# Local attention and a top-2 mixture of experts on one core: the normalisation after the product with v moves from VectorE to ScalarE and POOL, the row stores move to the sync queue, and the later steps come one turn later

## The chip, the core and the metric

The kernel runs on one core of a Trainium2 chip. The core has TensorE (PE; its weight loads are shown apart as PEld), VectorE (DVE), ScalarE (ACT), GpSimd (POOL) and SyncE (SP), which here only issues DMAs. Each engine works through its own list of instructions in order; DMAs are issued from the queues of SP, ACT and POOL. The metric is the device time of one execution in microseconds (us), the median of the runs.

## The reference

The inputs q, k, v have 8 batches, 8 heads, 576 positions and 64 values per head. Attention is local: each chunk of 64 positions attends to itself alone.

```python
scores = scale * np.matmul(q_c, k_c.transpose(0, 1, 2, 4, 3))
scores = scores - np.max(scores, axis=-1, keepdims=True)
attn = np.exp(scores)
attn = attn / (np.sum(attn, axis=-1, keepdims=True) + 1e-09)
out = np.matmul(attn, v_c)
```

The result, as 4608 token rows of 512 values (x), goes to a mixture of 8 experts. A noisy gate (`x @ w_gate + log1p(exp(x @ w_noise)) * noise`) picks two experts for each token and gives them softmax weights; each expert computes `relu(x @ w1[e]) @ w2[e]` on its tokens, and the weighted results are added to the output rows.

## The kernel before, in words

**Attention.** The 4608 tokens are 36 tiles of 128. One call of `attend(it)` is one turn, and it works on several tiles at different steps. For tile t: `scores` (turn t) makes 32 small products of 64x64 in PSUM; `soft_max`, `soft_sub` (DVE) take the row maximum and subtract it, `soft_exp` (ACT) takes the exponential in place; `p_trans` (turn t+2) transposes the result on PE and ACT copies it to SBUF (tile `pts`); `pv` (turn t+3) multiplies by v in 32 small products into PSUM banks 3 and 4. A column of ones beside v gives the row sums, so each head has 65 columns. In turn t+4 the DVE normalises: `norm_a` adds 1e-9 to the 8 sums (L440), `norm_b` takes their reciprocals (L443), `norm_c` multiplies the 512 columns by them, from PSUM into the SBUF tile `xs` (L447). `x_trans` (turn t+5) issues the store of `xs` to the DRAM buffer `xbuf` from ACT's queue, transposes `xs` on PE (L455), and ACT copies the result (L456). Every four tiles `gate_mm` and `gate_sum` make the gate's logits, in the same PSUM banks 3 and 4, beside pv's product. The softmax leaves out the division, which `norm_c` does at the end.

**Order.** The program is written out by hand: the order of the calls in `attend` is the order of the instructions on each engine, and the framework adds the waits. In one turn the order is `p_trans`, `x_trans`, gate, `scores`, `norm_a/b/c`, route steps, `soft_max`, route steps, `soft_sub`, route steps, `soft_exp`, `pv`. Loads of q, k and v come through SP, several tiles ahead.

**Routing.** `route(g)` is a generator that chooses the experts for a group of 4 or 8 tiles and builds the experts' token lists. `step_route(n)` runs n of its steps, ten in a turn, so its small DVE, ACT, POOL and PE instructions lie between those of attention. Its last part makes, for each tile, one-hot matrices (`gohp` on POOL and ACT at L596 to L598, `geq` on DVE at L600, `grhs` on POOL at L604) and adds them up by matmuls (`place`, L588). When a group is done, `gather` fetches the rows of `xbuf` that one of the first three expert blocks needs (POOL queue, L236).

**Experts.** 24 blocks of up to about 400 tokens: `layer1` and `layer2`, each product as three fp32r matmuls of high and low parts (L301). The turns after the last scores (`tail`) run as hooks between the matmuls of the first block's `layer1`. In `layer2` of block 0 the hook turns the tokens of block 1 (`x_tile`, transposes at L284), fixed at its seventh group of three matmuls per tile. The output buffer is set to zero by 37 stores of 256 KB from SP (`zero_out`, L666), which must have landed before the first expert's result is added to it (L268).

Weights for expert 0 are split into high and low parts in eight of the turns (its 10, 11, 13, 14, 16, 17, 19, 20): ACT makes the high part (L135), POOL the low part (L136).

Of the kernel before, what the change touches and what calls it, by code (L numbers as in the profile page):

```python
# [8 lines left out]
FT = mybir.dt.float32  # L9
# [4 lines left out]
AF = mybir.ActivationFunctionType  # L14
OP = mybir.AluOpType
# [4 lines left out]
P = 128  # L20
NTOK = 4608
NT = NTOK // P
DM = 512
# [37 lines left out]
def kernel(ctx, tc, qT, kT, vh, wgn, noise, w1, w2, out, caps=CAPS):  # L61
    nc = tc.nc
# [4 lines left out]
    xbuf = dram.tile([NROWS, DM], FT, name="xbuf")  # L67
# [50 lines left out]
    def w_load(e, which, c):  # L118
        st = stage.tile([P, 1024], FT, name="st")
        staged[e, which, c] = st  # L120
        if which == 1:
            nc.sync.dma_start(st, w1v[ds(place[e], 1), c].rearrange("o j r f -> (o j) r f") if e else w1[e, c * P:(c + 1) * P, :])
        else:
            nc.sync.dma_start(st.rearrange("p (f n) -> p f n", f=2),
                              w2[ds(place[e], 1) if e else slice(0, 1), 2 * c * P:(2 * c + 2) * P, :]
                              .rearrange("o (f p) n -> p (o f) n", f=2))
# [295 lines left out]
    def p_trans(t):  # L422
        for hp in range(4):
            nc.tensor.transpose(PS[:, 2, hp * P:(hp + 1) * P], PR[t][:, hp * P:(hp + 1) * P], ident)  # L424
        PT[t] = work.tile([P, 4, P], FT, name="pts", bufs=3)
        nc.scalar.activation(PT[t].rearrange("p a b -> p (a b)"), PS[:, 2, :], AF.Copy)

    pvb = PS[:, 3:5, 0:260].rearrange("p b (g n) -> p b g n", n=65)
# [1 line left out]
    def pv(t):  # L430
        v = vb[t // 2]
        for hp in range(4):
            for h, c in HC:
                r, s = slice(h * 64, h * 64 + 64), slice(c * 64, c * 64 + 64)
                nc.tensor.matmul(PS[s, 3 + h, hp * 65:hp * 65 + 65], PT[t][r, hp, s], v[r, t % 2, c, hp, :],  # L435
                                 start=True, stop=True)

    def norm_a(t):
        RC[t] = work.tile([P, 2, 4, 1], FT, name="rc", bufs=2)
        nc.vector.tensor_scalar(RC[t], pvb[:, :, :, 64:65], 1e-9, None, op0=OP.add)  # L440

    def norm_b(t):
        nc.vector.reciprocal(RC[t], RC[t])  # L443

    def norm_c(t):
        XS[t] = work.tile([P, DM], FT, name="xs", bufs=4)
        nc.vector.tensor_tensor(by_head(XS[t]), pvb[:, :, :, 0:64], RC[t].to_broadcast([P, 2, 4, 64]), OP.mult)  # L447

    def x_trans(t):
        g, r = divmod(t, 4)  # L450
        if r == 0:
            XT[g] = gx.tile([P, ND, 4, P], FT, name="xt", bufs=1)
        nc.scalar.dma_start(xbuf[(t + 1) * P:(t + 2) * P, :], XS[t])
        for d in range(ND):
            nc.tensor.transpose(PS[:, 5, d * P:(d + 1) * P], XS[t][:, d * P:(d + 1) * P], ident)  # L455
        nc.scalar.activation(XT[g][:, :, r, :], PS[:, 5, :].rearrange("p (d n) -> p d n", d=ND), AF.Copy)  # L456
# [3 lines left out]
    def gate_mm(g):  # L460
        for d in range(ND):
            nc.tensor.matmul(PS[32 * d:32 * d + 32, 6, :], wg[:, d, :], XT[g][:, d], start=True, stop=True)  # L462
        LS[g] = gx.tile([P, 4, P], FT, name="ls", bufs=1)
        nc.scalar.activation(LS[g].rearrange("p a b -> p (a b)"), PS[:, 6, :], AF.Copy)
# [6 lines left out]
    def gate_sum(g):  # L471
        for r in range(4):
            nc.tensor.matmul(lg_at(4 * g + r), LS[g][:, r, :], sel, start=True, stop=True)  # L473
# [169 lines left out]
    def step_route(n):  # L643
        for _ in range(n):
            while routing:
                try:
                    next(routing[0])
                    break
                except StopIteration:
                    routing.pop(0)  # L650
# [17 lines left out]
    def attend(it):  # L668
        STEPS = 2 if it < 33 else 3
        if it % 2 == 0 and it >= 2 and it // 2 + 3 < NT // 2:  # L670
            load_q(it // 2 + 3)
            load_k(it // 2 + 3)
        if it in (4, 7, 10, 13):
            w_load(0, 1, (it - 4) // 3)
        if 0 <= it - 2 < NT:
            p_trans(it - 2)
        if 0 <= it - 5 < NT:
            x_trans(it - 5)
        if it - 7 >= 0 and (it - 7) % 4 == 3:
            gate_sum((it - 7) // 4)  # L680
        if it - 6 >= 0 and (it - 6) % 4 == 3:
            gate_mm((it - 6) // 4)
        if it < NT:
            scores(it)
        if 0 <= it - 4 < NT:
            norm_a(it - 4)
            norm_b(it - 4)
            norm_c(it - 4)
            step_route(3 * STEPS)
        if it - 7 >= 0 and (it - 7) % 4 == 3:  # L690
            if grp_of[it - 7] != grp_of.get(it - 6):
                routing.append(route(grp_of[it - 7]))
        if it < NT:
            mx = soft_max(it)
            step_route(STEPS)
            soft_sub(it, mx)
            step_route(STEPS)
            soft_exp(it)
        if 0 <= it - 3 < NT:
            pv(it - 3)  # L700
        if it % 2 == 1 and it >= 3 and (it - 3) // 2 + 4 < NT // 2:
            load_v((it - 3) // 2 + 4)
        if it in (10, 11, 13, 14, 16, 17, 19, 20):
            w_split(0, 1, *wq.pop(0), eng=nc.gpsimd)
        if it in (29, 31, 33, 35):
            w_load(0, 2, (it - 29) // 2)
# [15 lines left out]
        x_tile(0, k)  # L722


    tail = [NT + 1 + a for a in range(6)]

    def hook_tail(f, d):
        if d == 0 and f % 2 == 0 and f >= 2:
# [212 lines left out]
```

## Time and profile before

| | |
|---|---|
| median of 3 runs | 1022.05 us (1020.68 to 1023.5) |
| the profiled execution | 1018.32 us, span 1016.4 us, mean granted TensorE clock 0.981 |
| PE busy | 968.3 us (95% of the span) |
| DVE, ACT, POOL busy | 461.4, 299.6, 484.6 us |
| first scores matmul | 5.66 us |
| first expert matmul | 154.30 us |
| first layer 2 matmul | 190.09 us |

In a row of the timeline the first number is the start in us from the span's start, the second the duration in us, then engine, line, operation, output and inputs; a bracket gives how long the engine had been idle before it and what ended that. A row of a table by windows gives, for each stretch, the busy us of PE, PEld, DVE, ACT and POOL (instructions in parentheses), then the granted clock, the DMA engines' busy share and GB/s. In a row of groups of instructions the last column before the bar is the count; after it stand the total us and the mean ns of one.

### The profile page before, as it was taken

What the parts mean: (1) busy time and instruction counts of PE and PEld (TensorE: products, weight loads), DVE (VectorE), ACT (ScalarE), POOL (GpSimd) and SP (SyncE); (2) the same over time, 40 slices, a digit from 0 to 9 for tenths busy, and PEclk for the clock granted to TensorE, in tenths of its full rate; (3) what the DMA queues carried; (4) which work ended last, traced back from release to release, by engine and by line L of the source; (5) the groups of instructions that cost most, each with busy time, mean ns of one, the idle gap of its engine ahead of it and who ended that gap; (6) DMA issues with size and microseconds to landing.
All of it is one profiled execution on the core that took longest, in us unless ns stands there. A gap on an engine that the chain in (4) does not pass through costs nothing.

```text
span 1016.4 us, 18332 instructions
## 1 busy us (share of the span) xinstructions
PE 968.3 (95%) x7353; PEld 865.4 (85%) x7353; DVE 461.4 (45%) x1037; ACT 299.6 (29%) x649; POOL 484.6 (48%) x618
## 2 busy tenths in 40 slices
PE   6878888999999999999999999999999999999995
PEld 5667766988889899989998999899989998899984
DVE  5577765554525353335334533453345334434311
ACT  3466653331414132213221322232223221323100
POOL 1133432434677777347724783487248725711111
PEclk9799978999999999999999999999999999999998
DMA  9988891133251553245224532353344234412213
GB/s 368 387 312 276 297 392 73 42 79 94 61 132 45 120 157 63 39 104 157 63 36 100 156 68 45 95 160 65 56 107 134 59 60 106 138 13 29 32 22 42
DMA packets 51943, 121.51 MB, mean 120 GB/s; under 512 B 8288, under 2 KB 9184, under 8 KB 51856
## 3 DMA queue, kind: packets, MB, share of 16 engines
q0 software_dynamic: 20160, 38.69, 20.4%
q1 hardware_dynamic: 26512, 72.20, 19.7%
q10 hardware_dynamic: 5184, 9.44, 2.4%
q8 instruction: 58, 0.95, 0.4%
q14 instruction: 29, 0.24, 0.1%
HBM read 81.56 MB, written 38.73 MB: 118 GB/s over the span
## 4 chain that ended last, share of the span: by engine, by line
PE 90%; DVE 5%; ACT 1%; issue 1%; DMA 1%; POOL 0%; SPq 0%; DVEq 0%; ACTq 0%; POOLq 0%
PE PS L301 79%; PE PS L588 2%; PE PS L435 2%; PE PS L408 2%; PE PS L424 2%; PE PS L455 1%; DMA kb<-in_kT 1%; DVE xs L447 1%; PE PS L330 1%; DVE mx L412 1%; DVE pr L417 1%; PE PS L473 1%; PE PS L462 1%; PE PS L284 0%; DVE xl L292 0%
## 5 line engine op out<-in xcount | busy, mean ns | idle before, releaser
L256 POOL DMA_INDIRECT xg<-xbuf,piece x257 | 265.8, 1034 | 71.7 <-issue 65.1
L301 PE MATMUL PS<-xh,w1h 128*128 128x384 f32 (+2 forms) x768 | 263.2, 343 | 2.4 <-DVE xl L292 1.4
L301 PE MATMUL PS<-xl,w1h 128*128 128x384 f32 (+2 forms) x768 | 260.6, 339 | 0.3 <-DVE xl L292 0.3
L301 PE MATMUL PS<-xh,w1l 128*128 128x384 f32 (+2 forms) x768 | 260.8, 340 | 0.0
L268 POOL DMA_INDIRECT out<-o,lid x73 | 116.9, 1601 | 238.9 <-DVE o L339 222.8
L301 PE MATMUL PS<-w2h,hh 128*128 128x512 f32 x584 | 228.7, 392 | 0.0
L301 PE MATMUL PS<-w2h,hl 128*128 128x512 f32 x584 | 227.7, 390 | 0.0
L301 PE MATMUL PS<-w2l,hh 128*128 128x512 f32 x584 | 227.5, 390 | 0.0
L319 ACT ACTIVATE hh<-PS 128x384 fp32r<-128x384 f32 (+1 forms) x192 | 93.9, 490 | 363.7 <-PE PS L301 363.7
L320 DVE SCALAR_TENSOR_TENSOR hl<-PS,hh 128x384 fp32r<-128x384 f32 (+1 forms) x192 | 107.2, 559 | 195.4 <-ACT hh L319 195.4
L339 DVE TENSOR_SCALAR o<-PS,lwt 128x512 f32<-128x512 f32 x73 | 54.7, 750 | 229.7 <-PE PS L301 229.7
L301 PEld LDWEIGHTS PS<-xh,w1h 128*128 128x128 f32 x768 | 144.6, 188 | 5.9 <-DVE xl L292 1.7
L301 PEld LDWEIGHTS PS<-xl,w1h 128*128 128x128 f32 x768 | 144.5, 188 | 2.3 <-DVE xl L292 0.5
L301 PEld LDWEIGHTS PS<-xh,w1l 128*128 128x128 f32 x768 | 144.4, 188 | 1.0
L301 PEld LDWEIGHTS PS<-w2h,hl 128*128 128x128 f32 x584 | 109.2, 187 | 23.5
L301 PEld LDWEIGHTS PS<-w2h,hh 128*128 128x128 f32 x584 | 109.2, 187 | 23.1 <-issue 0.8
L301 PEld LDWEIGHTS PS<-w2l,hh 128*128 128x128 f32 x584 | 109.3, 187 | 22.4
L291 ACT ACTIVATE xh<-y 128x512 fp32r<-128x512 f32 x67 | 41.2, 615 | 104.3 <-DVE y L288 104.3
L292 DVE TENSOR_TENSOR xl<-y,xh 128x512 fp32r<-128x512 f32 x67 | 45.0, 671 | 48.1 <-ACT xh L291 48.1
L596 POOL TENSOR_SCALAR gohp<-row_p,gpf 128x128 f32<-128x128 f32 x36 | 24.0, 666 | 72.7 <-DVE gpf L580 54.7
L288 DVE STREAM_TRANSPOSE y<-xg 128x512 f32<-128x512 f32 x67 | 45.6, 681 | 3.0 <-DMA xg<-xbuf,piece 2.8
L408 PEld LDWEIGHTS PS<-kb,qp 64*64 64x64 f32 x1152 | 23.9, 155 | 25.6 <-DVE pr L417 11.4
(138 smaller groups left out, 816.3 us busy)
## 6 DMA issues: line engine op xcount, KB each, us to landing
st<-in_w SPq DMA_DIRECT2D x64, 512.0 KB, 4.5
out<-zero SPq DMA_DIRECT2D x37, 256.0 KB, 4.6
vb<-in_vh SPq DMA_DIRECT2D x18, 520.0 KB, 6.8
qp<-in_qT SPq DMA_DIRECT2D x18, 512.0 KB, 7.5
kb<-in_kT SPq DMA_DIRECT2D x18, 512.0 KB, 8.1
xbuf<-xs ACTq DMA_DIRECT2D x36, 256.0 KB, 5.6
xg<-xbuf,piece POOLq DMA_INDIRECT x257, 2.7
out<-o,lid POOLq DMA_INDIRECT x73, 4.8
```

Source lines behind the costliest of these rows:

```text
L256: nc.gpsimd.indirect_dma_start(out=XG[e, j][:, t * P:(t + 1) * P], out_offset=None, in_=xpieces, in_offset=bass.IndirectOffsetOnAxis(ap=pi ...
L268: s = nc.gpsimd.indirect_dma_start(out=to, out_offset=bass.IndirectOffsetOnAxis(ap=rows, axis=0), in_=o, in_offset=None, compute_op=OP.add)
L288: nc.vector.transpose(y[:, 0:4 * r], x[:, 0:4 * r])
L291: nc.scalar.activation(oh, src, AF.Copy)
L292: nc.vector.tensor_sub(ol, src, oh.bitcast(FT))
L301: nc.tensor.matmul(p, a, b, start=first and n == 0, stop=last and n == 2)
L319: nc.scalar.activation(hh[:, 0:m], p, AF.Relu)
L320: nc.vector.scalar_tensor_tensor(hl[:, 0:m], p, 0.0, hh[:, 0:m].bitcast(FT), op0=OP.max, op1=OP.subtract)
L339: nc.vector.tensor_scalar(o[0:r], p[0:r], weights_of(i, j)[0:r], None, op0=OP.mult)
L408: nc.tensor.matmul(PS[s, h, o:o + 64], q[r, t % 2, hp, s], k[r, t % 2, hp, s], start=True, stop=True)
L424: nc.tensor.transpose(PS[:, 2, hp * P:(hp + 1) * P], PR[t][:, hp * P:(hp + 1) * P], ident)
L596: nc.gpsimd.tensor_scalar(ohp[:, 0], row_p, pf[:, 0, 0, r:r + 1], None, op0=OP.is_equal)
```

## The change

ScalarE now copies the whole product with v (2 banks x 4 heads x 65 columns) from PSUM to an SBUF tile `xu` (`unload`), as its first step of the turn t+4. `norm_a` reads the sums from `xu`, `norm_b` takes reciprocals on DVE as before, and the multiplication by them is done on POOL, SBUF to SBUF (now `norm_b`'s second part). The store of `xs` is a step of its own (`x_store`, turn t+5), issued from SP. `x_trans`, `gate_sum`, `gate_mm` and the start of a group's routing come one turn later, so the tail has seven turns instead of six. Six of a turn's ten route steps now stand ahead of the normalisation instead of behind it. Buffers: `pts` 3 to 2, `xs` 4 to 3, `xu` 2.

```diff
-        PT[t] = work.tile([P, 4, P], FT, name="pts", bufs=3)
+        PT[t] = work.tile([P, 4, P], FT, name="pts", bufs=2)
...
+    def unload(t):
+        XU[t] = work.tile([P, 2, 4, 65], FT, name="xu", bufs=2)
+        nc.scalar.activation(XU[t], pvb, AF.Copy)
+
     def norm_a(t):
         RC[t] = work.tile([P, 2, 4, 1], FT, name="rc", bufs=2)
-        nc.vector.tensor_scalar(RC[t], pvb[:, :, :, 64:65], 1e-9, None, op0=OP.add)
+        nc.vector.tensor_scalar(RC[t], XU[t][:, :, :, 64:65], 1e-9, None, op0=OP.add)
+        nc.vector.reciprocal(RC[t], RC[t])
 
     def norm_b(t):
-        nc.vector.reciprocal(RC[t], RC[t])
-
-    def norm_c(t):
-        XS[t] = work.tile([P, DM], FT, name="xs", bufs=4)
-        nc.vector.tensor_tensor(by_head(XS[t]), pvb[:, :, :, 0:64], RC[t].to_broadcast([P, 2, 4, 64]), OP.mult)
+        XS[t] = work.tile([P, DM], FT, name="xs", bufs=3)
+        nc.gpsimd.tensor_tensor(by_head(XS[t]), XU[t][:, :, :, 0:64], RC[t].to_broadcast([P, 2, 4, 64]), OP.mult)
+
+    def x_store(t):
+        nc.sync.dma_start(xbuf[(t + 1) * P:(t + 2) * P, :], XS[t])
 
     def x_trans(t):
...
-        nc.scalar.dma_start(xbuf[(t + 1) * P:(t + 2) * P, :], XS[t])
...
+        if 0 <= it - 4 < NT:
+            unload(it - 4)
         if 0 <= it - 2 < NT:
             p_trans(it - 2)
-        if 0 <= it - 5 < NT:
-            x_trans(it - 5)
+        if 0 <= it - 6 < NT:
+            x_trans(it - 6)
+        if it - 8 >= 0 and (it - 8) % 4 == 3:
+            gate_sum((it - 8) // 4)
         if it - 7 >= 0 and (it - 7) % 4 == 3:
-            gate_sum((it - 7) // 4)
-        if it - 6 >= 0 and (it - 6) % 4 == 3:
-            gate_mm((it - 6) // 4)
+            gate_mm((it - 7) // 4)
         if it < NT:
             scores(it)
         if 0 <= it - 4 < NT:
+            step_route(3 * STEPS)
             norm_a(it - 4)
             norm_b(it - 4)
-            norm_c(it - 4)
-            step_route(3 * STEPS)
-        if it - 7 >= 0 and (it - 7) % 4 == 3:
-            if grp_of[it - 7] != grp_of.get(it - 6):
-                routing.append(route(grp_of[it - 7]))
+        if 0 <= it - 5 < NT:
+            x_store(it - 5)
+        if it - 8 >= 0 and (it - 8) % 4 == 3:
+            if grp_of[it - 8] != grp_of.get(it - 7):
+                routing.append(route(grp_of[it - 8]))
...
-    tail = [NT + 1 + a for a in range(6)]
+    tail = [NT + 1 + a for a in range(7)]
```

How it moves instructions is seen at three places.

On ACT, an early turn, before the routing starts, and the first row of the next. Before, a turn is exponential (`pr`), copy of the transposed probabilities (`pts`), issue of the row store, copy of the transposed rows (`xt`):

```order
L420 ACTIVATE pr<-pr 128x512
L426 ACTIVATE pts<-PS 128x512
L453 DMA xbuf<-xs 128x512
L456 ACTIVATE xt<-PS 128x4x128
L420 ACTIVATE pr<-pr 128x512
```

With the change:

```order
L420 ACTIVATE pr<-pr 128x512
L442 ACTIVATE xu<-PS 128x520
L426 ACTIVATE pts<-PS 128x512
L462 ACTIVATE xt<-PS 128x4x128
L420 ACTIVATE pr<-pr 128x512
```

The copy `xu` stands directly behind the exponential of the turn before, and the DMA issue has left this engine. On DVE, in the same turns, the rows were, before:

```order
L412 TENSOR_REDUCE mx<-PS 128x8
L417 TENSOR_TENSOR pr<-PS,mx 128x2x4x64
L440 TENSOR_SCALAR rc<-PS 128x8
L443 RECIPROCAL rc<-rc 128x8
L447 TENSOR_TENSOR xs<-PS,rc 128x2x4x64
L412 TENSOR_REDUCE mx<-PS 128x8
```

and are now:

```order
L412 TENSOR_REDUCE mx<-PS 128x8
L417 TENSOR_TENSOR pr<-PS,mx 128x2x4x64
L446 TENSOR_SCALAR rc<-xu 128x8
L447 RECIPROCAL rc<-rc 128x8
L412 TENSOR_REDUCE mx<-PS 128x8
```

The large multiplication is gone, and the first of the two small instructions now takes its input from `xu`, ahead of the next turn's maximum.

On PE, from the last `place` of the routing's fourth group (L588, now L594; it completes the token list of expert block 1) towards the transposes of that block's tokens (L284). Before, the rows behind the last `place` begin with

```order
L588 MATMUL PS<-grhs,gohp 128x160 x2
L301 MATMUL PS<-xh_2622,w1h_1114 128x384
L301 MATMUL PS<-xl_2623,w1h_1114 128x384
L301 MATMUL PS<-xh_2622,w1l_1115 128x384
L301 MATMUL PS<-xh_2622,w1h_1358 128x384
L301 MATMUL PS<-xl_2623,w1h_1358 128x384
L301 MATMUL PS<-xh_2622,w1l_1359 128x384
L301 MATMUL PS<-w2h_2778,hh_2624 128x512
L301 MATMUL PS<-w2l_2779,hh_2624 128x512
L301 MATMUL PS<-w2h_2778,hl_2625 128x512
```

and 18 more L301 rows follow before the transposes: 27 matmuls, 6 of layer 1 and 21 of layer 2. With the change it is

```order
L594 MATMUL PS<-grhs,gohp 128x160 x2
L301 MATMUL PS<-w2h_3059,hh_2675 128x512
L301 MATMUL PS<-w2l_3060,hh_2675 128x512
L301 MATMUL PS<-w2h_3059,hl_2676 128x512
L301 MATMUL PS<-w2h_3059,hh_2677 128x512
L301 MATMUL PS<-w2l_3060,hh_2677 128x512
L301 MATMUL PS<-w2h_3059,hl_2678 128x512
L301 MATMUL PS<-w2h_3134,hh_2679 128x512
L301 MATMUL PS<-w2l_3135,hh_2679 128x512
L301 MATMUL PS<-w2h_3134,hl_2680 128x512
L284 MATMUL PS<-ident,xg 128x128 x4
```

Since the routing runs one turn later and the transposes stand where they stood, 9 matmuls are left between the two.

On SP, at the end of attention. Before:

```order
L369 DMA qp<-in_qT 128x1024
L373 DMA kb<-in_kT 128x1024
L377 DMA vb<-in_vh 128x1040
L124 DMA st<-in_w 128x2x512 x4
L666 DMA out<-zero 128x512 x37
L793 TENSOR_LOAD order
```

With the change:

```order
L454 DMA xbuf<-xs 128x512 x2
L124 DMA st<-in_w 128x2x512
L454 DMA xbuf<-xs 128x512 x4
L672 DMA out<-zero 128x512 x19
L454 DMA xbuf<-xs 128x512
L672 DMA out<-zero 128x512 x18
```

The 36 row stores now stand between the loads, and the 37 zero stores stand behind all but one of them.

More of the change, by code (lines that the diff above doesn't have):

```diff
@@ L436, in pv @@
                                  start=True, stop=True)
+    XU = {}
+    def unload(t):
+        XU[t] = work.tile([P, 2, 4, 65], FT, name="xu", bufs=2)
+        nc.scalar.activation(XU[t], pvb, AF.Copy)
     def norm_a(t):
         RC[t] = work.tile([P, 2, 4, 1], FT, name="rc", bufs=2)
-        nc.vector.tensor_scalar(RC[t], pvb[:, :, :, 64:65], 1e-9, None, op0=OP.add)
+        nc.vector.tensor_scalar(RC[t], XU[t][:, :, :, 64:65], 1e-9, None, op0=OP.add)
+        nc.vector.reciprocal(RC[t], RC[t])
     def norm_b(t):
-        nc.vector.reciprocal(RC[t], RC[t])
-    def norm_c(t):
-        XS[t] = work.tile([P, DM], FT, name="xs", bufs=4)
-        nc.vector.tensor_tensor(by_head(XS[t]), pvb[:, :, :, 0:64], RC[t].to_broadcast([P, 2, 4, 64]), OP.mult)
+        XS[t] = work.tile([P, DM], FT, name="xs", bufs=3)
+        nc.gpsimd.tensor_tensor(by_head(XS[t]), XU[t][:, :, :, 0:64], RC[t].to_broadcast([P, 2, 4, 64]), OP.mult)
+    def x_store(t):
+        nc.sync.dma_start(xbuf[(t + 1) * P:(t + 2) * P, :], XS[t])
     def x_trans(t):
```

## The prediction

> **What bounds the kernel now.** I read the page's busy shares and slices first, then a table of windows cut at the starts of DVE's maximum (one a turn), then the timeline of single turns.
>
> ```profile
> span 1016.4 us, 18332 instructions
> ...
> PE   6878888999999999999999999999999999999995
> PEclk9799978999999999999999999999999999999998
> ```
>
> From the seventh slice on (one is 25.4 us) PE is full: nothing of this change runs there, and what attention gains or loses shifts the rest as a whole. The change is worth what it does in the first 200 us.
>
> ```profile
> core 0: us, PE busy (x) PEld busy (x) DVE busy (x) ACT busy (x) POOL busy (x), PEclk, DMA share, GB/s
> 17.85:55.10 37.25, 31.59 (x752) 26.00 (x744) 23.48 (x51) 18.71 (x35) 3.14 (x3) 0.86 1.01 393
> 73.41:91.75 18.34, 17.50 (x378) 14.47 (x376) 13.76 (x34) 14.28 (x35) 12.85 (x18) 1.00 0.72 240
> 91.75:111.57 19.82, 14.74 (x386) 12.01 (x385) 17.29 (x73) 11.07 (x28) 4.02 (x6) 1.00 0.82 283
> 60.40:67.51 7.11, 5.53 (x148) 3.90 (x141) 6.88 (x41) 2.73 (x6) 0.00 (x0) 1.00 0.97 341
> 126.17:133.42 7.25, 4.60 (x117) 2.97 (x115) 6.78 (x34) 2.83 (x5) 3.12 (x3) 1.00 1.05 394
> 133.42:141.16 7.74, 6.97 (x118) 6.39 (x118) 4.30 (x20) 3.22 (x8) 0.34 (x1) 0.59 1.03 395
> ```
>
> There are three kinds of turn. The ten light ones (17.85 to 55.10, before routing) are PE's, slowed by a granted clock of 0.86. Where `place` runs (73.41 to 91.75) PE is 95% busy. Nine turns in which the routing chooses experts (60.40 to 67.51, 91.75 to 111.57, 126.17 to 133.42; 34.18 us together) are DVE's: 6.88 of 7.11, 17.29 of 19.82, 6.78 of 7.25 us busy. There the multiplication that leaves DVE should be worth most.
>
> **The change part by part.** *A new cycle through ACT.* One light turn:
>
> ```profile
> 20.44 0.69 DVE L412 TENSOR_REDUCE mx<-PS 128x8 f32<-128x512 f32 x1
> 21.24 0.69 DVE L417 TENSOR_TENSOR pr<-PS,mx 128x512 f32<-128x512 f32 x1
> 21.85 0.16 DVE L440 TENSOR_SCALAR rc<-PS 128x8 f32<-128x8 f32 x1
> 21.97 0.63 ACT L420 ACTIVATE pr<-pr 128x512 f32<-128x512 f32 x1 [0.99 <-DVE pr L417]
> 22.28 0.69 DVE L447 TENSOR_TENSOR xs<-PS,rc 128x512 f32<-128x512 f32 x1
> 22.50 0.58 ACT L426 ACTIVATE pts<-PS 128x512 f32<-128x512 f32 x1
> 22.89 0.68 DVE L412 TENSOR_REDUCE mx<-PS 128x8 f32<-128x512 f32 x1
> 25.86 0.69 DVE L412 TENSOR_REDUCE mx<-PS 128x8 f32<-128x512 f32 x1 [0.46 <-PE PS L408]
> ```
>
> Maximum follows maximum after 2.45 and 2.97 us. With the change the copy `xu` stands on ACT behind the exponential, the sums on DVE wait for `xu`, and the next maximum stands behind the sums. So no turn is shorter than: maximum to subtraction 0.80 (20.44 to 21.24), subtraction 0.69, hand-over 0.04 (21.93 to 21.97), exponential 0.63, the copy 0.60 (an estimate: `pts`, 512 columns from PSUM, takes 0.58, and `xu` has 520), two hand-overs of 0.04, and sums and reciprocals 0.43 (21.85 to 22.28): 3.27 us. Queued behind the waiting sums are the maximum, the subtraction and every route step of DVE; PE's scores of the next tile wait for that subtraction. Which turns feel it? Those now under 3.27:
>
> ```profile
> 17.85 0.69 DVE L412 TENSOR_REDUCE mx<-PS 128x8 f32<-128x512 f32 x1 [0.44 <-PE PS L408]
> 30.30 0.69 DVE L412 TENSOR_REDUCE mx<-PS 128x8 f32<-128x512 f32 x1 [1.92 <-PE PS L408]
> 33.41 0.69 DVE L412 TENSOR_REDUCE mx<-PS 128x8 f32<-128x512 f32 x1 [0.59 <-PE PS L408]
> 44.95 0.69 DVE L412 TENSOR_REDUCE mx<-PS 128x8 f32<-128x512 f32 x1 [1.74 <-PE PS L408]
> 47.65 0.69 DVE L412 TENSOR_REDUCE mx<-PS 128x8 f32<-128x512 f32 x1 [0.17 <-PE PS L408]
> ```
>
> 17.85 to 20.44 (2.59), the two above, 30.30 to 33.41 (3.11) and 44.95 to 47.65 (2.70): they lose 0.68 + 0.82 + 0.30 + 0.16 + 0.57 = 2.5. The high halves of the expert weights, which ACT copies behind the exponential in eight turns, enter the cycle too, 0.62 each:
>
> ```profile
> L135 ACT ACTIVATE w1h<-st 128x512 fp32r<-128x512 f32 x8 | 4.9, 617 | 0.0
> L136 POOL TENSOR_TENSOR w1l<-st,w1h 128x512 fp32r<-128x512 f32 x8 | 10.3, 1286 | 60.9 <-ACT w1h L135 60.9
> L604 POOL TENSOR_TENSOR grhs<-geq,vals 128x320 f32<-128x320 f32 x20 | 14.4, 720 | 0.4 <-DVE rc L440 0.3
> ```
>
> About one of the three in light turns counts, 0.5. Sum **+3.0**; bounds 0 (waits of PE already cover it) and +6 (ten turns of 0.6).
>
> *DVE's relief.* The nine DVE turns lose 9 x 0.69 = 6.2 of DVE work. But the cycle with about 0.3 of route steps between maximum and subtraction is 3.57, and one of these turns has a weight copy: 9 x 3.57 + 0.6 = 32.7 against 34.18, a gain of 1.5. Something goes back, at SBUF:
>
> ```profile
> 111.34 0.32 DVE L600 TENSOR_TENSOR geq<-row_je,gpf 128x160 f32<-128x160 f32 x1
> 113.92 0.72 POOL L604 TENSOR_TENSOR grhs<-geq,vals 128x320 f32<-128x320 f32 x1
> 114.18 0.64 DVE L600 TENSOR_TENSOR geq<-row_je,gpf 128x160 f32<-128x160 f32 x1
> ```
>
> The same DVE instruction takes 0.32 alone and 0.64 when it starts within a POOL instruction: it ends 0.18 behind POOL's end (114.64). The multiplication on POOL starts as DVE goes over to the maximum, and I cost it like L136 (two SBUF inputs, 512 columns): 1.29; `grhs` scaled from 320 columns gives 1.15. A route step with two SBUF inputs behind the maximum then ends at 1.29 + 0.18 = 1.47 instead of 0.69 + 0.32 = 1.01: 0.45 more, in perhaps two of the nine turns, 1.0. The term is **-0.5**; bounds -6.2 (no cycle) and +3.
>
> *POOL where `place` runs.* Its 12.85 us grow by 5 x 1.29 to 19.3, against 18.34 of the stretch. The product on POOL has a turn of slack (its readers stand two turns later), which hides about half: **+0.5**; bounds 0 and +2.6. ACT grows by 5 x 0.60 to 17.3 and stays under it.
>
> *Routing's start.* pv waits for the five activations with which a group's routing opens:
>
> ```profile
> PEld PS L435 <- ACT gz L495: 3.6, 3, 2.1
> ```
>
> They come behind `xu` now, 0.60 later, three times in attention: at most 1.8, taken **+1.0**, since pv is not always the last to arrive.
>
> *The zero stores.* They flood the DMA queues late in attention, and ACT, which issues the row stores, stands for it:
>
> ```profile
> 119.81 0.33 SPq L666 DMA_DIRECT2D out<-zero  x1
> 134.52 0.60 ACT L456 ACTIVATE xt<-PS 128x512 f32<-128x512 f32 x1 [1.82 <-DMA out<-zero]
> 139.10 0.60 ACT L456 ACTIVATE xt<-PS 128x512 f32<-128x512 f32 x1 [2.40 <-DMA out<-zero]
> 150.01 2.68 SPq L666 DMA_DIRECT2D out<-zero  x3
> ```
>
> Behind the row stores on SP the zeros start after attention, and ACT no longer issues stores. The turn 133.42 to 141.16 lasted 7.74 at a clock of 0.59; at least the wait of 1.82 + 2.40 can go, and at the full clock some 3 us of PE's 6.97. But the low clock came after PE's thin turns (4.60 busy of 7.25), and these remain. I take **-2.5**; bounds 0 and -5. The 37 stores then need about 33 us (119.81 to 152.7) from some 156 on; the first expert result is added at 198.06, so they stay hidden; without that cover up to 5 us would be lost.
>
> *Loads and stores on one queue.* Two loads of 512 KB a pair of turns stand behind a store that waits for POOL; they are issued six turns before use, so one turn later costs nothing, and the DMAs' share of 1.01 up to 55.10 is the same bytes in another order.
>
> *The token list of block 1.*
>
> ```profile
> 188.50 0.70 PE L588 MATMUL PS<-grhs,gohp 128*128 128x160 f32 x4
> 189.25 0.32 DVE L622 TENSOR_TENSOR acc<-acc,PS 128x160 f32<-128x160 f32 x1 [0.40 <-PE PS L588]
> 190.85 1.05 POOL L236 DMA_INDIRECT xg<-xbuf,lid  x1 [4.96 <-DVE lid L207]
> xg<-xbuf,lid POOLq DMA_INDIRECT x3, 3.4
> 194.90 0.60 PE L284 MATMUL PS<-ident,xg 128*128 128x128 f32 x4
> 198.06 1.65 POOL L268 DMA_INDIRECT out<-o,lid  x1 [3.58 <-DVE gex L527]
> ```
>
> From the end of the last `place` (189.20) the list, the gather's issue at 190.85 and 3.4 to landing end at 194.25: 5.05 us, which 27 matmuls just covered (the transposes began at 194.90). Now 9 matmuls of layer 2 stand there. A `place` and its 27 take 194.90 - 188.50 = 6.40; nine take about a third of the rest, 2.0. PE must wait 5.05 - 2.0 = 3.0: **+3.0**; bounds +2.5 and +4.7 (if the clock drops to half for one 3.4 us window, 1.7).
>
> The Trainium skill ("TensorE: Matmul & The Clock Gate", Part 1) says that the clock falls to half after an idle window of about 3.4 us. The stall is just under that, so by this rule the clock holds and the term stays 3.0.
>
> Sum: 3.0 - 0.5 + 0.5 + 1.0 - 2.5 + 3.0 = **+4.5**. The profiled execution took 1018.32 (span 1016.4 and 1.9 around it), 3.7 below the median; it becomes 1022.8, and the median 1022.05 + 4.5 = 1026.5.
>
> **The rivals.** *Faster: the copy is free.* ACT waited for DVE's subtraction 44.1 us in attention, so it has room:
>
> ```profile
> ACT pr L420 <- DVE pr L417: 44.1, 25, 6.3
> ```
>
> If the copy fits there and the cycle does not bind, the relief counts in full (-6.2), the zeros give all (-5), the other attention terms are 0 and the gather costs 3.0: -8.2, 1013.9. Against it stands the order: that room lies before the exponential, the copy behind it. Chance 0.2.
>
> *Slower: POOL and DVE hold each other up in every route turn.* If the 0.45 above falls in all of the some 22 turns with route steps, it is 9.9 instead of 1.0: 1035.4. It decides where the step behind the maximum has two SBUF inputs. For it: 0.64 against 0.32. Against: in turns that PE fills, DVE's delay is hidden, and many steps read one input. Chance 0.2. The Trainium skill ("SBUF — State Buffer", SBUF: two separate sides) has the rule behind it: VectorE with two SBUF inputs and GpSimd share a port pair, and whoever starts first holds it to the end of its instruction. The end 0.18 after POOL's agrees.
>
> *Slower: the stores.* `xs` has 3 buffers, and its store lies behind loads while the DMAs are full. If a store lands a turn late, POOL, then `xu`, then pv wait, some 3 us twice: 1032. Chance 0.05.
>
> *No change*: the cycle is hidden behind PE's own waits and only the gather and the zeros count, +0.5: 1022.6. Chance 0.1.
>
> **How the numbers follow.** The forecast has 0.45. A difference of 0.3%, 3.07 us, is about what a measurement tells from none. Of the forecast's own range, 1022 to 1031, a third lies within it: slower 0.30 + 0.2 + 0.05 = 0.55, the same 0.15 + 0.1 = 0.25, faster 0.2. The range over all cases, 1014 to 1036, leaves the ends of both rivals out.
>
> **What would show it.** Right: maxima of light turns 3.2 to 3.4 apart, with DVE's sums waiting for ACT `xu`; PE waiting some 3 us at L284 near 190; no zero store before 150. Wrong: DVE's sums never waiting for `xu`, or light turns still at 2.5 to 2.9 (then the faster rival); `geq` of 0.6 and more in most route turns (the port); sums waiting for POOL or DMA (the stores).

## The result: slower by 1.2 to 1.5%

The changed kernel takes 1033.68 us (median; 1032.25 to 1035.78), the kernel before beside it 1021.37 (1018.85 to 1023.5): ratio 1.0123, 95% interval 1.0093 to 1.0153, or 12.3 us more. A second comparison gave 1036.44 (ratio 1.0147, 1.0124 to 1.0170). The forecast was 1026.5, in a range of 1014 to 1036.

### The profile page after: what moved, and what is told of

The parts are those of the page before. It is cut to its first block, busy times and chain, and to the rows that moved or that the text cites. A ratio compares the mean times of both kernels' runs of the same rounds, so it can differ in the third digit from the quotient of the medians.

```text
span 1031.7 us, 18427 instructions
## 1 busy us (share of the span) xinstructions
PE 976.8 (95%) x7353; PEld 869.0 (84%) x7353; DVE 449.7 (44%) x1001; ACT 318.0 (31%) x685; POOL 518.0 (50%) x654
## 4 chain that ended last, share of the span: by engine, by line
PE 87%; DVE 5%; ACT 3%; issue 2%; DMA 1%; POOL 0%; SPq 0%; ACTq 0%; DVEq 0%; POOLq 0%
PE PS L301 78%; PE PS L594 2%; PE PS L408 2%; DVE pr L417 1%; DVE mx L412 1%; PE PS L435 1%; ACT xu L442 1%; PE PS L330 1%; PE PS L479 1%; PE PS L424 1%; DMA xg<-xbuf,lid 1%; PE PS L461 1%; PE PS L468 1%; DVE rc L446 0%; PE PS L284 0%
## 5 line engine op out<-in xcount | busy, mean ns | idle before, releaser
L256 POOL DMA_INDIRECT xg<-xbuf,piece x257 | 262.5, 1022 | 77.0 <-issue 69.9
L301 PE MATMUL PS<-xh,w1h 128*128 128x384 f32 (+2 forms) x768 | 262.1, 341 | 1.4 <-DVE xl L292 1.4
L301 PE MATMUL PS<-xl,w1h 128*128 128x384 f32 (+2 forms) x768 | 260.4, 339 | 0.3 <-DVE xl L292 0.3
L301 PE MATMUL PS<-xh,w1l 128*128 128x384 f32 (+2 forms) x768 | 260.4, 339 | 0.0
L301 PE MATMUL PS<-w2h,hh 128*128 128x512 f32 x584 | 230.2, 394 | 0.0
L301 PE MATMUL PS<-w2h,hl 128*128 128x512 f32 x584 | 229.0, 392 | 0.0
L301 PE MATMUL PS<-w2l,hh 128*128 128x512 f32 x584 | 228.9, 392 | 0.0
L301 PEld LDWEIGHTS PS<-xh,w1h 128*128 128x128 f32 x768 | 144.2, 188 | 4.9 <-DVE xl L292 1.6
L301 PEld LDWEIGHTS PS<-xl,w1h 128*128 128x128 f32 x768 | 144.2, 188 | 2.3 <-DVE xl L292 0.5
L301 PEld LDWEIGHTS PS<-xh,w1l 128*128 128x128 f32 x768 | 144.3, 188 | 1.0
L301 PEld LDWEIGHTS PS<-w2h,hl 128*128 128x128 f32 x584 | 109.9, 188 | 23.8
L301 PEld LDWEIGHTS PS<-w2h,hh 128*128 128x128 f32 x584 | 109.9, 188 | 23.4 <-issue 0.8
L301 PEld LDWEIGHTS PS<-w2l,hh 128*128 128x128 f32 x584 | 109.9, 188 | 22.6
L451 POOL TENSOR_TENSOR xs<-xu,rc 128x512 f32<-128x512 f32 x36 | 37.9, 1052 | 69.6 <-ACT pts L426 38.2
```

What stands on the lines that cost most here:

```text
L256: nc.gpsimd.indirect_dma_start(out=XG[e, j][:, t * P:(t + 1) * P], out_offset=None, in_=xpieces, in_offset=bass.IndirectOffsetOnAxis(ap=pi ...
L301: nc.tensor.matmul(p, a, b, start=first and n == 0, stop=last and n == 2)
L451: nc.gpsimd.tensor_tensor(by_head(XS[t]), XU[t][:, :, :, 0:64], RC[t].to_broadcast([P, 2, 4, 64]), OP.mult)
```

## The profile after

The page of the changed kernel (span, and PE's busy tenths in 40 slices):

```profile
span 1031.7 us, 18427 instructions
...
PE   6879888899999999999999999999999999999995
```

Nothing shows there: the slices read like those before. The stages have to be compared by events that both kernels have. In the table, each from one profile (us from the span's start), "last maximum" is DVE's maximum of the 36th tile, and the results are the first, third and seventh addition of an expert's rows to the output. The kernel before has three profiles: its own, a repeat, and the experiment with stores on SP, which runs in the same time.

| | last maximum | first expert matmul | third result | seventh result |
|---|---|---|---|---|
| before | 144.06 | 154.30 | 210.96 | 281.37 |
| before, repeat | 143.20 | 152.87 | 207.88 | 278.40 |
| before, stores on SP | 144.18 | 153.85 | 208.68 | 278.75 |
| changed | 151.55 | 162.55 | 221.11 | 293.19 |
| changed, repeat | 152.87 | 163.06 | 221.69 | 293.28 |
| changed, transposes later | 150.63 | 159.28 | 211.26 | 285.12 |
| changed, gate's sum first | 146.13 | 155.43 | 212.41 | 283.58 |
| both of these | 147.29 | 157.22 | 210.60 | 283.70 |
| both, and normalisation behind the subtraction | 147.24 | 157.43 | 210.91 | 284.74 |
| before, only later steps | 143.56 | 152.44 | 212.14 | 284.32 |
| before, only the new normalisation | 157.68 | 167.82 | 222.53 | 292.71 |
| before, gate's sum first | 142.34 | 152.00 | 206.47 | 278.64 |
| the same, small matmuls in two runs | 140.32 | 149.98 | 204.54 | 275.01 |

Means of the first three rows against the changed kernel (up to the first expert matmul the row "transposes later" is the same program and counts with it): attention up to the last maximum 143.8 against 151.7, **+7.9**; from there to the first expert matmul 9.9 against 9.9; from there to the third result 55.5 against 58.6, **+3.1**; to the seventh 70.3 against 71.8, **+1.5**. Together 12.5, about the measured difference.

In attention PE now waits for the copy `xu` in three places. PE's waits of the changed kernel up to 162 us (us in total, times, longest):

```profile
PE PS L479 <- ACT xu L442: 7.6, 7, 2.1
PE PS L408 <- DVE pr L417: 6.4, 9, 1.5
...
PE PS L435 <- ACT xu L442: 3.3, 7, 1.0
...
PE PS L435 <- ACT gz L501: 1.4, 2, 1.2
PE PS L539 <- ACT xu L442: 1.2, 2, 1.0
```

L479 is the gate's sum (L473 before), which the prediction priced nowhere. It writes its 16 columns a tile into PSUM bank 3 or 4, beside the product that `xu` reads, and it stands behind `xu` in the program; so it waits for the copy, seven times. The chain of one such turn, without routing, on the changed kernel's timeline (the rows beside the chain are left out):

```profile
38.48 0.69 DVE L412 TENSOR_REDUCE mx<-PS 128x8 f32<-128x512 f32 x1 [0.82 <-PE PS L408]
...
39.21 0.69 DVE L417 TENSOR_TENSOR pr<-PS,mx 128x512 f32<-128x512 f32 x1
...
39.94 0.63 ACT L420 ACTIVATE pr<-pr 128x512 f32<-128x512 f32 x1 [0.94 <-DVE pr L417]
40.47 0.61 ACT L135 ACTIVATE w1h<-st 128x512 fp32r<-128x512 f32 x1
...
40.99 0.58 ACT L442 ACTIVATE xu<-PS 128x520 f32<-128x520 f32 x1
...
41.63 1.06 PE L479 MATMUL PS<-sel,ls 128*128 128x16 f32 x8 [1.71 <-ACT xu L442]
...
42.62 0.69 PE L408 MATMUL PS<-kb,qp 64*64 64x64 f32 x32
...
43.38 0.69 DVE L412 TENSOR_REDUCE mx<-PS 128x8 f32<-128x512 f32 x1 [1.30 <-PE PS L408]
```

Everything is in one line: maximum, subtraction, exponential, the high part of a weight (L135), copy, the gate's sum (PE idle for 1.71), the next scores, the next maximum, 4.90 us later. Before, DVE's sums stood behind the gate's sum, and PE went on to the scores.

## The experiments

**The changed kernel again.**

> The changed kernel once more, for a second profile and more times. Theory A (its losses are the program's): PE waits 7 to 8 us for xu in front of the gate's sum and 3 to 4 us for the gather, the first expert matmul stands at 158 to 164, the median is 1032 to 1036. Theory B (a good part is chance of the execution): one of these is missing, or the median is under 1031.

Measured: 1036.44 (1032.74 to 1037.34); PE waits 8.7 us for `xu` at the gate's sum and 3.75 for the gather, the first expert matmul starts at 163.06. The losses are the program's.

**The gate's sum ahead of the copy.**

```diff
+        if it - 8 >= 0 and (it - 8) % 4 == 3:
+            gate_sum((it - 8) // 4)
         if 0 <= it - 4 < NT:
             unload(it - 4)
...
-        if it - 8 >= 0 and (it - 8) % 4 == 3:
-            gate_sum((it - 8) // 4)
```

> The changed kernel with the gate's sum (gate_sum) ahead of the copy xu in the turn instead of behind it; nothing else moves. Theory A (seven times PE stands 1 to 2 us in front of the gate's sum because xu reads the same PSUM banks first, 7.6 us in all): that wait is gone from the table of PE's waits, attention ends 4 to 7 us earlier, median 1027 to 1030. Theory B (the cycle through ACT and the clock set the turn anyway): the wait reappears in front of pv or of the scores, median 1032 to 1034.

Measured: 1030.78 (1029.03 to 1031.93), ratio 1.0096 (1.0079 to 1.0112), a little above theory A's 1027 to 1030. From the same turn:

```profile
38.55 0.69 DVE L412 TENSOR_REDUCE mx<-PS 128x8 f32<-128x512 f32 x1 [0.82 <-PE PS L408]
39.12 0.97 PEld L479 LDWEIGHTS PS<-sel,ls 128*128 128x128 f32 x8 [0.30 <-ACT ls L470]
...
41.03 0.69 PE L408 MATMUL PS<-kb,qp 64*64 64x64 f32 x32
...
41.06 0.58 ACT L442 ACTIVATE xu<-PS 128x520 f32<-128x520 f32 x1
...
41.68 1.12 DVE L446 TENSOR_SCALAR rc<-xu 128x8 f32<-128x8 f32 x1 [1.71 <-ACT xu L442]
...
42.96 0.64 DVE L412 TENSOR_REDUCE mx<-PS 128x8 f32<-128x512 f32 x1
```

The gate's sum runs in the shadow of the maximum, and the scores start at 41.03 instead of 42.62. With this order the last maximum stands at 146.13, 147.29 and 147.24 (three kernels), mean 146.9 against 151.7: this order gives back **4.8** of attention's 7.9. The wait in front of the gate's sum is gone; of its 7.6 us, 2.9 are back in front of pv, as theory B has it (for `gz` 3.0 instead of 1.4, for `xu` 4.6 instead of 3.3). The same move also made the kernel before 1.5 and 3.5 us earlier at the last maximum (the last two rows of the table, mean 141.3 against 143.8). So not all of the 4.8 is due to the change, and with the gate's sum first in both kernels 5.6 us are left in attention. The execution's time fell by less than the stages at 283 us (9.6 earlier there); where the rest went is told under "small matmuls" below.

**The two small instructions behind the subtraction,** on top of the gate's sum first and the later transposes, so that the maximum no longer stands behind `xu` (in the changed kernel `norm_a` holds the sums and the reciprocals and `norm_b` the product on POOL, which moves along):

```diff
             step_route(3 * STEPS)
-            norm_a(it - 4)
-            norm_b(it - 4)
+            if it >= NT:
+                norm_a(it - 4)
+                norm_b(it - 4)
...
             soft_sub(it, mx)
+            if it >= 4:
+                norm_a(it - 4)
+                norm_b(it - 4)
             step_route(STEPS)
```

> The changed kernel with the gate's sum first and block 1's transposes later, and now also with the two small instructions of the normalisation (and POOL's product) behind the subtraction of the same turn instead of ahead of the maximum, so that DVE's maximum no longer stands behind the copy xu. Theory A (the cycle maximum, subtraction, exponential, xu, sums, maximum sets the light turns at 2.88 us): turns 4 to 6 fall from 2.88 to 2.3 to 2.7, the first expert matmul from 155.4 to 157.2 down to 152 to 154.5, median 1023 to 1026. Theory B (the light turns are set by PE and its own waits for xu in front of pv): turns stay at 2.8 to 2.9, median 1026 to 1029.

Measured: ratio 1.0061 (1.0041 to 1.0081); without this edit it was 1.0061 (1.0037 to 1.0085). (Only the ratios compare: in this last comparison the kernel before itself took 1015.49.) Turns 4 to 6 last 2.31, 2.80 and 3.60 us instead of 2.88 each, 8.7 together as before. DVE's waits up to 162 us, without and with the edit:

```profile
DVE rc L446 <- ACT xu L442: 30.3, 26, 1.7
DVE mx L412 <- PE PS L408: 15.8, 15, 4.2
```

```profile
DVE mx L412 <- PE PS L408: 47.6, 28, 4.3
...
DVE rc L446 <- ACT xu L442: 1.0, 1, 1.0
```

The 30.3 us of waiting for `xu` went, and the maximum waits 31.8 us more for PE's scores. Neither theory came out as written. Over the whole of attention nothing is gained (last maximum 147.24, without the edit 147.29), but not evenly: the 21st maximum stands at 77.7, against 80.0 and 80.5 in the two kernels with the gate's sum first and the old place, and the 29th at 114.1, against 111.8 and 112.3. Between the two, 6.8 us of this execution ran at half clock, and none of the other two. So breaking the cycle brought nothing that can be seen in the time; whether the cycle alone costs up to 2.8 us, which another loss here took back, stays open.

**Only the new normalisation** (copy, product on POOL) in the kernel before, with no step later and the stores on ACT's queue:

```diff
+        if 0 <= it - 4 < NT:
+            unload(it - 4)
         if 0 <= it - 2 < NT:
             p_trans(it - 2)
...
-            norm_c(it - 4)
```

(`norm_a` and `norm_b` are those of the changed kernel, `pts` has 2 buffers, `xs` 3.)

> The kernel before with the new normalisation alone: copy xu on ACT at the head of the turn, sums and reciprocals on DVE from xu, product on POOL; stores from ACT's queue, gate, routing and tail as before, no step later. Theory A (the copy xu costs attention its time: PE stands at the gate's sum behind xu, and thin PE windows halve the clock): the first expert matmul at 158 to 162, no wait for the gather, median 1026 to 1030. Theory B (later steps and the sync queue cost it): first expert matmul within 1.5 of 154.3, median 1020 to 1024.

Measured: 1037.26, ratio 1.0147 (1.0123 to 1.0171). The first expert matmul starts at 167.82, 14 us late, which is worse than theory A. PE's waits up to 162 us:

```profile
PE PS L459 <- POOL xs L451: 7.3, 11, 1.6
...
PE PS L477 <- ACT xu L442: 5.1, 5, 1.7
```

(L459 are the transposes of `xs`, L477 the gate's sum.) The copy and POOL make the product late for the next turn; with the later steps that wait is 0.3 in the changed kernel. So this normalisation makes use of the later steps in attention; what they cost lies behind it. (The changed kernel differs from this one also by the sync queue and by six route steps ahead of the normalisation; the place of the route steps was not tried alone.)

**The product on DVE instead of POOL,** from `xu`:

```diff
-        nc.gpsimd.tensor_tensor(by_head(XS[t]), XU[t][:, :, :, 0:64], RC[t].to_broadcast([P, 2, 4, 64]), OP.mult)
+        nc.vector.tensor_tensor(by_head(XS[t]), XU[t][:, :, :, 0:64], RC[t].to_broadcast([P, 2, 4, 64]), OP.mult)
```

> The changed kernel with the multiplication by the reciprocals on DVE (from xu, SBUF to SBUF) instead of on POOL. Theory A (POOL has room and holds DVE up little): DVE's turns get 0.7 longer, median 1034 to 1039. Theory B (POOL and DVE hold each other up, or the product on POOL comes late): DVE's steps beside it get shorter, median 1028 to 1032.

Measured: 1049.42, ratio 1.0268 (1.0251 to 1.0285), worse than either bound. Once the copy is made, POOL is the better place by 13 to 16 us. The edit differs from the kernel before by the copy, the later steps, the place of the route steps and the sync queue, and loses 28 us against it, which was not taken apart.

**Only the stores on SP.** The kernel before with `nc.scalar.dma_start(xbuf...)` as `nc.sync.dma_start`, at the same place.

> The kernel before with only the row stores moved to the sync queue, at the same place (turn t+5), so that the zero stores stand behind them. Theory A (the zero stores cost attention about 2.5 us): no ACT wait for out<-zero, first expert matmul 1 to 3 us earlier than the 152.9 and 154.3 of the two profiles before, median 1018 to 1020. Theory B (loads behind stores on one queue give it back): first expert matmul within 1 of 153.6, median 1020 to 1023.

Measured: 1021.46, ratio 1.0001 (0.9983 to 1.0018); ACT no longer waits for a zero store, and the first expert matmul is at 153.85. Theory B: worth nothing.

**Only the later steps.** The kernel before with `x_trans(it - 6)`, `gate_mm` and `gate_sum` on `it - 7` and `it - 8`, the routing on `it - 8`, seven turns of tail; DVE normalises from PSUM, ACT issues the store in turn t+5.

> The kernel before with the later steps alone: x_trans, gate and routing one turn later, the store of xs where it was (ACT's queue, turn t+5), the normalisation on DVE as before. Theory A (later steps cost only behind attention, at the gather): the first expert matmul within 1.5 us of 154.3, PE waits 3 to 4 us for the gather, median 1024 to 1027. Theory B (they also lengthen attention): first expert matmul at 157 or later, median 1028 or more.

Measured: 1026.5 (1024.83 to 1030.79), ratio 1.0053 (1.0033 to 1.0073). The first expert matmul stands at 152.44, as before; PE waits 3.09 us for the gather, and the third result comes 59.7 us after the first expert matmul instead of 55.5. Theory A.

**The transposes of block 1 later,** alone, and with the gate's sum first.

```diff
+        LATE1 = ((1, 4), (1, 7), (2, 6))
...
-            if i == 0 and f == 6 and k < len(nxt):
-                x_tile(1, k)
+            if i == 0 and (k, f) in LATE1:
+                x_tile(1, LATE1.index((k, f)))
```

> The changed kernel with the transposes of block 1's tokens 18 matmuls later in layer 2 of block 0 (first tile after 13 groups of three instead of 7, the second 3 groups on). Theory A (PE waits 3.77 us for the gather and then runs one window at half clock, 1.7 us): both go, and the median falls by 3 to 5, to 1029 to 1031. Theory B (the wait is only handed on, because layer 1 of block 1 then waits for the same tokens): 1033 to 1034.

> The changed kernel with both edits: the gate's sum ahead of xu, and the transposes of block 1's tokens 18 matmuls later. Theory A (these two are the cost that can be mended): first expert matmul near 155.4 as with the first edit alone, no wait of 3 us for the gather, third expert result added at 207 to 209 (210.96 before), median 1025 to 1029, above before only by what the small matmuls of expert 1 lose. Theory B (the wait is handed on): 1030 to 1034.

Measured alone: 1034.5 (1028.89 to 1037.38), ratio 1.0132 (1.0114 to 1.0151): in time no difference from the changed kernel that could be told, with a spread of 8.5 us. The profile does show what was expected: the wait goes from 3.77 to 0.3, and first expert matmul to third result takes 52.0 instead of 58.6; 2.07 of it comes back as a wait for the next gather, and by the seventh result 4.6 are left. With the gate's sum first: 1027.61, ratio 1.0061 (1.0037 to 1.0085), against 1.0096 without the later transposes. Together the two edits take back about half of the loss, clear of noise. One by one it is less sure: the gate's sum first is clear in time only against the second comparison of the changed kernel (1.0147), and the gain from the later transposes shows in the profile's stages, not clearly in time. The other half, some 6 us, is not traced to a cause.

**Small matmuls: how much is chance.** From the seventh result to the end the profiles differ by up to 8.5 us, most of it at one place and with no wait that names a cause: expert 1's last tile, 128 small matmuls (L330).

> The kernel before once more, for a second profile. In the profiles so far the first run of small matmuls of 32 rows (expert 1's last tile, 128 matmuls) takes 3.63 us before, 6.20 with the change, and 9.0 to 10.6 in the experiments, with PE waiting for nothing that the profile shows; the same code in experts 2 to 4 always takes 1.88 for half as many. Theory A (the kernel's code decides): 3.6 again, within 0.3. Theory B (chance of the single execution): another value between 3.6 and 11, and the time moves with it.

Measured: 1022.86 (ratio 1.0014, 0.9997 to 1.0031). The place in the first profile of the kernel before, and in the repeat:

```profile
330.19 3.70 PE L330 MATMUL PS<-st,hf 128*32 128x128 f32 x128
```

```profile
327.13 2.08 PE L330 MATMUL PS<-st,hf 128*32 128x128 f32 x62
329.54 0.43 PE L330 MATMUL PS<-st,hf 128*32 128x128 f32 x4 [0.33 <-issue]
330.28 0.44 PE L330 MATMUL PS<-st,hf 128*32 128x128 f32 x6 [0.31 <-issue]
...
333.98 2.55 PE L330 MATMUL PS<-st,hf 128*32 128x128 f32 x41 [0.34 <-issue]
```

The same program took 3.70 us there once and 9.40 the other time (327.13 to 336.53): theory B. Profiles gave 6.27 and 8.91 for the changed kernel, 10.69 with the gate's sum first, 3.70 with the normalisation behind the subtraction. The time of a single profile can therefore be 6 us less or more by chance, and stages are compared ahead of this place.

**The gate's sum first in the kernel before,** where DVE's sums stood behind it (15.1 us in 8 times):

```diff
+        if it - 7 >= 0 and (it - 7) % 4 == 3:
+            gate_sum((it - 7) // 4)
         if 0 <= it - 2 < NT:
             p_trans(it - 2)
...
-        if it - 7 >= 0 and (it - 7) % 4 == 3:
-            gate_sum((it - 7) // 4)
```

> The kernel before with the gate's sum at the head of the turn, ahead of the transposes. DVE's sums stood 14.6 us behind the gate's sum there (7 times), because both use the same PSUM banks. Theory A (this wait sets those turns): attention 2 to 5 us shorter, median 1016 to 1020. Theory B (the turn ends with PE anyway, and the gate's sum only waits for its own input ls at the new place): within 1 of before, 1020 to 1023.

Measured: 1019.94, ratio 0.9987 (0.9971 to 1.0003). The last maximum is 1.5 us earlier here and 3.5 in the next experiment, which has the same attention; in time it is not clear of nothing.

**And the small matmuls in two runs,** on top of it: `tail2` takes a list of its 32-row pieces, and `layer2` calls it for the first ahead of the block's tiles and for the second behind the first of them.

> The kernel before with the gate's sum at the head of the turn, and with expert 1's two runs of 64 small matmuls (the last tile's 32 rows each) apart: one where both stood, the other behind the next tile of layer 2. Theory A (256 PE instructions in 3.6 us are more than the supply of instructions delivers; 128 in a row always took 1.88): each of the two takes 1.9 to 2.5 us, and the median falls by 3 to 6 against the 1019.9 with the gate's sum alone, to 1014 to 1017. Theory B (something else at this place slows PE, say POOL's gathers): the two take 7 to 10 us together again, median 1018 to 1022.

Measured: 1017.0 (1013.52 to 1020.0), ratio 0.9962 (0.9943 to 0.9980): faster than both kernels. The second run takes 1.95 us as theory A has it, the first 4.14: after 45 matmuls it still falls into groups of six or seven, some 0.75 us apart. Together that is 6.1, between the two theories. Whether the split itself helps is not settled: the intervals with and without it overlap, the place takes 3.7 to 10.7 us by chance anyway, and in this profile the first expert matmul came 2.0 us earlier than in the one without the split, by the same program. What stands is that this version is 0.4% faster than the kernel before.

## Why the prediction was right and where it failed

The direction held, slower was the likeliest, and so did the range, if barely: the second comparison's median, 1036.44, lies just above its end of 1036. The size did not hold: +4.5 where 12.3 and more was measured. That the range reached so far was in part luck, for its upper end came from the rival with the ports, and the gate's sum, the largest of PE's waits in attention, is in no term. By its steps:

- **The new cycle** (+3.0). It exists, and shorter than worked out: three light turns alike at 2.88, not 3.27.

```profile
20.75 0.64 DVE L412 TENSOR_REDUCE mx<-PS 128x8 f32<-128x512 f32 x1
...
21.43 0.69 DVE L417 TENSOR_TENSOR pr<-PS,mx 128x512 f32<-128x512 f32 x1
22.15 0.63 ACT L420 ACTIVATE pr<-pr 128x512 f32<-128x512 f32 x1 [1.27 <-DVE pr L417]
22.69 0.59 ACT L442 ACTIVATE xu<-PS 128x520 f32<-128x520 f32 x1
23.30 0.17 DVE L446 TENSOR_SCALAR rc<-xu 128x8 f32<-128x8 f32 x1 [1.19 <-ACT xu L442]
23.51 0.20 DVE L447 RECIPROCAL rc<-rc 128x8 f32<-128x8 f32 x1
23.63 0.64 DVE L412 TENSOR_REDUCE mx<-PS 128x8 f32<-128x512 f32 x1
```

  Instructions on one engine start before the last has ended: `xu` 0.54 behind the start of an exponential of 0.63, the maximum 0.12 behind a reciprocal of 0.20. Durations and hand-overs were added up where, on one engine, starts are what counts. And the term is about 1 at most, not +3.0: turns 4 to 6 take 8.64 us together, against 8.01, 8.83 and 8.97 in the three profiles before, and the light turns end (15th maximum) at 54.5, against 55.1, 52.8 and 53.2. With the cycle broken they end at 52.8, against 53.9 and 54.0 with only the gate's sum first. The step "which turns feel it? Those now under 3.27" took one profile's short turns for the rule.

- **The missing step.** "Routing's start" looked at pv behind the five activations (+1.0; PE's wait for `gz` is 1.4, it was 1.2; with the gate's sum first it is 3.0 in the changed kernel and in the kernel before) and not at what else uses pv's two banks. The gate's sum was in the rows of before, as what DVE's sums waited for. With the copy ahead of it the order of the two turned round, and PE, not DVE, is the one that waits: 7.6 us, of which the other order gave back 4.8. This is the largest part of the loss that an experiment gave back, with the reserve that the same move is worth 1.5 to 3.5 in the kernel before.

- **DVE's relief** (-0.5). The place of the give-back was right and its reach was not. DVE's groups in the stretch from the 11th to the last maximum, before and changed:

```profile
L447 DVE TENSOR_TENSOR xs<-PS,rc 128x512 f32<-128x512 f32 x26 | 18.0, 691 | 0.9
...
L600 DVE TENSOR_TENSOR geq<-row_je,gpf 128x160 f32<-128x160 f32 x20 | 7.6, 384 | 0.1
...
L440 DVE TENSOR_SCALAR rc<-PS 128x8 f32<-128x8 f32 x25 | 4.0, 159 | 12.2 <-PE PS L473 10.3 <-PE PS L435 1.9
...
L521 DVE TENSOR_TENSOR goh<-row,gmi 128x64 f32<-128x64 f32 x4 | 0.9, 220 | 0.1
...
L521 DVE TENSOR_TENSOR goh<-row,gmi 128x32 f32<-128x32 f32 x2 | 0.4, 187 | 0.0
```

```profile
L446 DVE TENSOR_SCALAR rc<-xu 128x8 f32<-128x8 f32 x25 | 10.2, 407 | 19.6 <-ACT xu L442 19.6
L606 DVE TENSOR_TENSOR geq<-row_je,gpf 128x160 f32<-128x160 f32 x19 | 9.6, 532 | 0.1
...
L527 DVE TENSOR_TENSOR goh<-row,gmi 128x64 f32<-128x64 f32 x4 | 2.2, 577 | 0.1
...
L527 DVE TENSOR_TENSOR goh<-row,gmi 128x32 f32<-128x32 f32 x2 | 0.9, 464 | 0.0
```

  18.0 us left DVE and 10.0 came back (`rc` 6.2, `geq` 2.0, `goh` 3.1 against 1.3), most of it in `rc`, which reads one input from SBUF, where the prediction counted only steps with two. What of attention's remaining 3.1 us (146.9 against 143.8; 5.6 with the gate's sum first in both) is due to this was not told apart. The rival with the ports had 9.9 us of such delay and came near the time (1035.4), but part of the measured loss has other causes, the gate's sum and the gather; how much of the 10.0 us of DVE became time stays open. The rival in which the copy is free and the relief counts fell.

- **POOL in place's stretch** (+0.5): the product takes 1.05 us, not the 1.29 of L136, and PE waits for it 0.3 us in all. Nothing.

- **The zero stores** (-2.5): 0, by the experiment with the stores on SP. The 4.2 us of ACT waiting for `out<-zero` stood in one profile; the repeat of the same kernel has none, and its last maximum comes only 0.9 us earlier. A wait of an engine with room was read as time.

- **The gather** (+3.0): the cause is right, and so is the size by the third result, +3.1; that the size fits so well is partly luck. The wait is 3.77 and 3.75; the clock, too, did what only the bound allowed for (below), and a wait of 0.96 for `xh` that stood there before is gone. Moving the transposes took 6.6 us off this stage in the changed kernel and 3.6 off with the gate's sum first. The prediction's first reading, that nothing of this change runs from the seventh slice on, leaves out this very wait, which lies in the eighth. The 1.5 up to the seventh result is new, in part a wait for the next gather (0.44 and 1.58 us), and no larger than the difference between the last two rows of the table there (72.2 and 70.5), which have the same program up to that point; no experiment was made on it alone.

- **Stores and loads on one queue** (0, and a rival of 1032): POOL waited 4.2 us for a store in two turns, and nobody behind it on PE's path. (The loads are three for a pair of turns, 512, 512 and 520 KB, not two.) The rival did not come.

## What to carry to other kernels

When a read of PSUM moves to another engine, list everything that writes or reads the same banks and look at who now waits for whom: a good part of the loss here was not in the copy but in a small matmul beside it that stood behind the copy in the program, and one line's move gave 4.8 of attention's 7.9 us back. The same move should be tried in the kernel before as well, or its gain is put down to the change alone. Moving work off the engine that is full pays only as far as the engine that takes it doesn't hold the first up, and a wait that goes at one place can come back at another: 30.3 us of waiting for `xu` went, and 31.8 came back in front of the maximum. And two profiles of the same kernel should be read before a term is built on a wait that stands in one.

## What the runs showed of the hardware

**The granted clock goes in fixed windows of 3.41 us.** In every profile all stretches at half clock start and end on one grid of 3.413 us, and last 3.41, 6.83 or 10.24. In the changed kernel and in the one with the product on DVE, the windows around the gather's wait:

```profile
197.46:200.88 3.42, 2.29 (x11) 1.53 (x9) 1.31 (x7) 0.00 (x0) 1.28 (x2) 1.00 0.99 384
200.88:204.29 3.41, 0.77 (x6) 0.76 (x7) 0.00 (x0) 0.10 (x1) 1.74 (x3) 1.00 0.77 243
204.29:207.71 3.42, 3.42 (x10) 2.64 (x9) 2.79 (x17) 0.49 (x1) 0.87 (x1) 0.50 0.14 55
```

```profile
215.04:218.45 3.41, 2.21 (x10) 1.46 (x9) 1.32 (x7) 0.00 (x0) 1.34 (x2) 1.00 0.89 344
218.45:221.86 3.41, 1.52 (x9) 1.38 (x10) 0.23 (x1) 0.60 (x1) 1.70 (x3) 1.00 0.69 190
221.86:225.28 3.42, 3.42 (x17) 2.82 (x16) 3.32 (x28) 0.00 (x0) 1.62 (x2) 1.00 0.13 46
```

The wait of 3.77 us left 0.77 us of work in one window, and the next ran at half clock; the one of 3.08 straddled a border and left 2.21 and 1.52, and the clock stayed. Each half-clock stretch up to 300 us in the first profiles of the two kernels began behind a window in which PE was busy for 0.23 to 0.67 of the time; others with 0.55 to 0.67, and the one of 1.52 us above (0.45), were followed by the full clock, so PE's busy share alone does not decide. The Trainium skill ("TensorE: Matmul & The Clock Gate", Part 1) has the free-running window of 3413 ns, with which the grid agrees; but the prediction took its idle window for one that has to be empty, and here windows with PE busy for up to 0.67 of the time stood ahead of the half clock. Up to 300 us the kernel before ran 30.7 and 13.6 us at half clock in its two profiles, the changed one 44.4 and 37.5, and with the gate's sum first 20.5 and, with the later transposes too, 27.3: a part of the thin waits seems to be paid twice.

**A small DVE instruction with one SBUF input ends behind POOL.** From the changed kernel's timeline:

```profile
46.06 1.28 POOL L136 TENSOR_TENSOR w1l<-st,w1h 128x512 fp32r<-128x512 f32 x1 [2.02 <-ACT w1h L135]
46.51 0.86 DVE L446 TENSOR_SCALAR rc<-xu 128x8 f32<-128x8 f32 x1 [1.71 <-ACT xu L442]
```

Eight sums a row, mostly 0.17 us, end here 0.03 us behind POOL's end (47.37 and 47.34). Nine of the 36 take 0.28 us and more, up to 1.59, and end 0.02 to 0.04 behind POOL's end. Five of the nine stand behind the low parts of the weights (L136), which POOL made before as well, and with the product on DVE seven still do: it is the sums' new source that brings them there, not the product on POOL alone. From PSUM the same instruction took 0.145 to 0.167 us in all 36 cases. The Trainium skill ("SBUF — State Buffer", SBUF: two separate sides) names, beside two SBUF inputs, an instruction in a two-port mode. These rows agree with a wait for POOL's end; that the instruction is in such a mode no run here shows.

**PE's small matmuls run short of something that no row names:** in most of the slow cases the profile has groups of three to seven of them, some 0.74 us apart, after the first 31 to 63 of 128 in a row, and the 128 take 3.70 us in some executions and up to 10.69 in others, of the same program 3.70 and 9.40.
